# Chunked attention into a bilinear network: values, scores and sums of three units in one run on TensorE

## The chip, the cores and the metric

The kernel runs on one core of a Trainium2 chip. The metric is device time in microseconds (us) of one execution; the median of several runs is compared. Below, "the profile" is one execution recorded instruction by instruction, with times in us from the start of its span.

## What is computed

The reference, cut to what matters (8 batches, 8 heads, 576 tokens each, head size 64; 4608 tokens in all, model width 512, inner width 1536):

```python
# attention inside chunks of 64 tokens
scores = (1 / sqrt(64)) * q_c @ k_c.T            # per head and chunk, 64 x 64
attn = exp(scores - max) ; attn /= attn.sum(-1)
x = (attn @ v_c), heads side by side             # 4608 x 512
# bilinear network
a = x @ w_a ; b = x @ w_b                        # 512 x 1536 each
out = (a * b) @ w_out                            # 4608 x 512
```

## The kernel before, in words

**Blocks, units, groups.** The tokens are cut into 9 blocks of 512 (K = 0 to 8), each of two units of 256 tokens (U = 0 to 17; block K has units 2K and 2K+1). Attention is done unit by unit, the network block by block. Blocks 0 and 1 take their own path at the start; from block 2 on each block goes through six groups (K,i), i = 0 to 5, one for each 256 columns of w_a and w_b. The order of every engine's instructions is written out by hand in the program: what follows in the text follows in the engine's queue.

**Attention of a unit** has four steps. `scores` (L266): 64 small matmuls (64x64) on the transposed q and k in `qkt` into two banks of PSUM, then Exp on ScalarE into `E` (of the two Exp the first follows at once, the second is put off to `exps`). `sums` (L296): four matmuls with a stationary block of ones give the sum over each chunk, spread over the rows; ScalarE takes Ln into `ln`. `inverse` (L317): ScalarE takes exp(-ln), one instruction over 128x1024. `values` (L324): 64 small matmuls of v and E; VectorE multiplies by the inverse and writes x (tile `xT`, L344). These small matmuls use quarters of TensorE's array (64*64 in the profile); all others use the whole array (128*128). The banks of values and of sums come from the pool `pt` by default; scores may be given a pool.

**A group** makes a and b for 256 columns with seven products in place of eight (a Strassen-Winograd scheme): p1, p6, p2, p5, p7, p3, p4 (L460 to L493), each four matmuls of 128x256 (`product`, L446). p1 fills bank A (pool `pa`); ScalarE copies A into bank B (`pb`, two banks in turn, L464); p6 adds to B, ScalarE copies B to u; p2 adds to A, copied to b; p5 adds to B, copied to v (L457). p7 fills C (`pc`). Then `add7` (VectorE, L484 and L485): c = C + v, and C = C + u in PSUM. p3 adds to B, and VectorE multiplies B by b; p4 adds to C, and VectorE multiplies C by c (L496); the products a*b go to `ab_sb`. The products need sums and differences of weights (t1 to t4) and of x (s1 to s4, `combine_x`, L412, four VectorE instructions a block: s1 and s2 and s3 and s4).

p3 and p4 of a group are issued during the next one, so TensorE's order in the loop (L892 to L935) is: p1 of this group, an out part, p3 of the last, p6 of this, p4 of the last, p2 of this, an out part, p5, p7. Attention steps stand in two places, after p3 (`attend(K, i, 0)`) and before p5 (`attend(K, i, 1)`); the table `attention` (L845 to L872) says which step where.

**The output of a block** (`OutGroup`, L537) is made in the next block by the same scheme: parts n0 to n6, each in two halves (th = 0, 1) of six matmuls. n0 and n1 fill bank A (`po`), copied to bank B (`pq`) by ScalarE after n0 and scaled into the first half of o0 after n1 (L612); n2, n3 and n5 add to B, which goes to u, v and the second half of o0 (L617, L620, L624); n4 and n6 fill C (`po`): after n4 VectorE scales C + v into o1 and then adds u to C in PSUM (L637, L641), after n6 it scales C into o1 (L630). `chunks` (L879) says how many halves stand in each of a group's two places. They need sums of `ab_sb`, made by `combine_ab` (L508) on GpSimd: three parts for each of j = 0, 1, 2 (j = 0 in group 4, j = 1 in group 5, j = 2 in group 0 of the next block), then part 3 for all j.

**Inputs.** `bring(U)` (L363): GpSimd casts q and k of unit U, SP issues the loads of the next unit and then the transposing DMAs of q and k into `qkt`, GpSimd casts v. SP also issues the stores. The staging tiles have 8 buffers, `raw`, `qkt` 3, `E`, `ln` and the out tiles 2.

Of the kernel before, what the change touches and what calls it, by code (L numbers as in the profile page):

```python
# [16 lines left out]
def kernel(  # L17
# [275 lines left out]
            late.pop(0)()  # L293
            n -= 1

    def sums(U, halves=None):  # L296
        E = E_of[U]
        sm = [bank() for _ in range(2)]
        for cl in range(2):
            for j in range(2):  # L300
                nc.tensor.matmul(  # L301
                    sm[cl][j * 64:j * 64 + 64, :],
                    ones[cl * 64:cl * 64 + 64, :],
                    E[cl * 64:cl * 64 + 64, j].rearrange("p m g s -> p (m g s)"),
                    start=True,
                    stop=True,
                )
        ln_of[U] = sm_pool.tile([128, 2, NKT, 128], FP32, name="ln")
        rs_of[U] = ln_of[U]
        for cl in range(2):  # L310
            nc.scalar.activation(
                out=ln_of[U][:, cl].rearrange("p m n -> p (m n)"), in_=sm[cl], func=AF.Ln
            )
            if halves:
                inverse(U, cl)

# [43 lines left out]
        if f is not None:  # L360
            values(f)

    def bring(U):  # L363

        if U >= NU:
            return
        cast(U, "qk")
        load(U + 1, "q" if U < 9 else "qkv")
        transpose_dma(U)
        bring_v(U)  # L370

    def bring_v(U):
        cast(U, "v")
        if U < 9:
            load(U + 1, "kv")
# [33 lines left out]

    s_of = {}  # L410

    def combine_x(K, parts=(0, 1, 2, 3)):  # L412
        xT = x_tiles[K]
        x11, x12 = xT[:, 0:2, 0:256], xT[:, 2:4, 0:256]
        x21, x22 = xT[:, 0:2, 256:512], xT[:, 2:4, 256:512]
        if K not in s_of:
            s_of[K] = [s_pool.tile([128, 2, 256], FP16, name=f"s{j}") for j in range(1, 5)]
        s1, s2, s3, s4 = s_of[K]
        for part in parts:
            o, x0, x1, op = (  # L420
                (s1, x21, x22, ADD),
                (s2, s1, x11, SUB),
                (s3, x11, x21, SUB),
                (s4, x12, s2, SUB),
            )[part]
            nc.vector.tensor_tensor(out=o, in0=x0, in1=x1, op=op)

    class Group:

# [107 lines left out]
    class OutGroup:  # L537
# [20 lines left out]
        def part(self, n, th):  # L558
# [28 lines left out]
            for cols in (slice(0, 128), slice(128, 256)) if end else [slice(0, 256)]:  # L587
                for kt in range(HFT):
                    nc.tensor.matmul(  # L589
                        t[:, c0:c0 + 256][:, cols],  # L590
                        a[:, kt, th * 128:th * 128 + 128],
                        w[:, kt, cols],
                        start=n in (0, 4) and first and kt == 0,
                        stop=last and kt == HFT - 1,
                        skip_group_check=True,
                    )
                if end:
                    nc.vector.tensor_scalar(
                        out=rows(self.o1, cols), in0=self.C[:, cols], scalar1=OUT_SCALE,
                        scalar2=None, op0=MULT,  # L600
                    )
                    store(
                        self.K, 1, th, self.o1[:, th], cols, nc.scalar if cols.start else nc.sync
                    )
            if not last or end:
                return
            if n == 0:
                self.B = self.bank(1)
                nc.scalar.copy(out=self.B, in_=self.A)
            elif n == 1:  # L610
                self.o0 = self.tile_of(0)
                nc.scalar.activation(  # L612
                    out=rows(self.o0, lo), in_=halves(self.A), func=AF.Copy, scale=OUT_SCALE
                )
            elif n == 2:
                self.u = self.temp("uo_sb")
                nc.scalar.copy(out=self.u, in_=self.B)  # L617
            elif n == 3:
                self.v = self.temp("vo_sb")
                nc.scalar.activation(out=self.v, in_=self.B, func=AF.Copy, scale=OUT_SCALE)  # L620
            elif n == 4:
                self.o1 = self.tile_of(1)
            elif n == 5:
                nc.scalar.activation(  # L624
                    out=rows(self.o0, hi), in_=halves(self.B), func=AF.Copy, scale=OUT_SCALE
                )
                for c in [th] if one else range(2):
                    store(self.K, 0, c, self.o0[:, c])
            else:
                nc.vector.tensor_scalar(  # L630
                    out=rows(self.o1, lo), in0=halves(self.C), scalar1=OUT_SCALE,
                    scalar2=None, op0=MULT,
                )
                for c in [th] if one else range(2):
                    store(self.K, 1, c, self.o1[:, c], lo if one else slice(0, DM))
            if n == (3 if one else 4):
                nc.vector.scalar_tensor_tensor(  # L637
                    out=rows(self.o1, hi), in0=halves(self.C), scalar=OUT_SCALE,
                    in1=halves(self.v), op0=MULT, op1=ADD,
                )  # L640
                nc.vector.tensor_tensor(out=self.C, in0=self.C, in1=self.u, op=ADD)  # L641
                if one:
                    store(self.K, 1, th, self.o1[:, th], hi)

# [27 lines left out]
    with tc.manual_schedule(  # L672
# [174 lines left out]
        def at(K, i, n, f, u):  # L847
            if u < NU:
                attention.setdefault((K, i, n), []).append(lambda: f(u))

        def scores_beside(pool):
            return lambda u: scores(u, (pool, psum_b[0]), 1)

        for K in range(2, NBLK):
            U = 2 * K + 2
            if K == 2:
                at(K, 0, 0, lambda u: combine_x(2, (2, 3)), U)
                at(K, 0, 0, scores, U)
                at(K, 0, 1, sums, U)
            else:  # L860
                attention[K, 0, 0] = [lambda K=K: combine_x(K, (2,))]
                attention[K, 0, 1] = [lambda K=K: combine_x(K, (3,))]
                at(K, 0, 0, sums, U)
            at(K, 1, 0, inverse, U)
            at(K, 2, 1, values, U)
            at(K, 2, 1, scores_beside(psum_o), U + 1)
            at(K, 3, 0, sums, U + 1)
            at(K, 3, 1, inverse, U + 1)
            at(K, 4, 1, values, U + 1)
            at(K, 4, 1, scores_beside(psum_q), U + 2)  # L870
            at(K, 5, 0, lambda u: combine_x(u // 2, (0,)), U + 1)
            at(K, 5, 1, lambda u: combine_x(u // 2, (1,)), U + 1)  # L872

        def attend(K, i, n):
            for f in attention.get((K, i, n), ()):
# [2 lines left out]
        last = None  # L878
        chunks = {  # L879
            2: (1, 1, 1, 1, 1, 2, 1, 2, 3, 0, 1, 1),  # L880
            4: (1, 1, 1, 1, 2, 1, 1, 2, 2, 0, 1, 1),
            NBLK - 1: (1,) * 12,
        }

# [7 lines left out]
        for K in range(2, NBLK):  # L892
            for i in range(NWP):
                if i == (2 if K == 2 else 1):
                    for j in range(3):
                        combine_ab(K - 1, 3, j)
                if i == 1:
                    bring(2 * K + 4)
                elif i == 3 and K > 2:
                    bring(2 * K + 5)  # L900
                elif i == 3:
                    cast(9, "qk")
                    load(10)
                    transpose_dma(9)
                if i == 0:
                    g = OutGroup(K - 1)
                    outs += [
                        lambda g=g, n=n, th=th: g.part(n, th) for n in range(7) for th in range(2)
                    ]
                now = Group(K, i)  # L910
                now.p1()
                if last:
                    last.add7()
                chunk(chunks.get(K, chunks[4])[2 * i])
                if K == 2 and i == 0:
                    for j in range(3):
                        combine_wo(3, j)
                if last:
                    last.p3()
                attend(K, i, 0)  # L920
                now.p6()
                if last:
                    last.p4()
                    finish(last)
                if K == 2 and i < 3:
                    combine_w(i + 3, 3)
                if K == 2 and i == 4:
                    cast(9, "v")
                now.p2()
                chunk(chunks.get(K, chunks[4])[2 * i + 1])  # L930
                attend(K, i, 1)
                now.p5()
                exps()
                now.p7()
                last = now  # L935
        ends = [
# [46 lines left out]
```

The softmax here doesn't subtract the row's maximum and nothing guards it: scores larger than these inputs give would overflow.

## Time and profile before

| | us |
|---|---|
| median of 8 runs (lowest, highest) | 303.99 (303.34, 306.97) |
| the profiled execution's own time | 304.43 |
| its span | 302.6 |
| TensorE busy in the span | 292.9 |
| VectorE, ScalarE, GpSimd busy | 210.1, 196.3, 192.4 |
| mean granted TensorE clock | 0.994 of full speed |
| mean of one: p1 to p7 matmul (128x256) | 0.273 |
| ScalarE copy of a bank (L457, `u_sb`) | 0.588 |
| VectorE multiply out of a bank (L496) | 0.689 |
| GpSimd `combine_ab` (first part) | 1.182 |

A timeline line gives start, duration, engine, line of the program, operation, what is written <- what is read, shapes and count, and in brackets how long the engine was idle before it and what ended that. Instructions on one engine overlap a little at their ends, so the distance of two starts can be less than the first one's duration; a matmul's end is modelled, and the distance of starts is its cost. PE is TensorE, DVE VectorE, ACT ScalarE, POOL GpSimd, SPq the queue of DMA issues on SP. Six groups make a block, some 30 us: block 5 begins near 172, block 6 near 202.

### The profile page before, as it was taken

What the parts mean: (1) busy time and instruction counts of PE and PEld (TensorE: products, weight loads), DVE (VectorE), ACT (ScalarE), POOL (GpSimd) and SP (SyncE); (2) the same over time, 40 slices, a digit from 0 to 9 for tenths busy, and PEclk for the clock granted to TensorE, in tenths of its full rate; (3) what the DMA queues carried; (4) which work ended last, traced back from release to release, by engine and by line L of the source; (5) the groups of instructions that cost most, each with busy time, mean ns of one, the idle gap of its engine ahead of it and who ended that gap; (6) DMA issues with size and microseconds to landing.
All of it is one profiled execution on the core that took longest, in us unless ns stands there. A gap on an engine that the chain in (4) does not pass through costs nothing.

```text
span 302.6 us, 8607 instructions
## 1 busy us (share of the span) xinstructions
PE 292.9 (97%) x3525; PEld 232.4 (77%) x3527; DVE 210.1 (69%) x343; ACT 196.3 (65%) x355; POOL 192.4 (64%) x180
## 2 busy tenths in 40 slices
PE   6799999999999999999999999999999999999995
PEld 2344567766588888888888888888888888888884
DVE  3457767858567696769667966786679667965773
ACT  2643567358487768776867687768776876566622
POOL 0567657999799488818881888179717901780650
PEclk9899999999999999999999999999999999999999
DMA  7999999989999979899859386948723001100024
GB/s 226 283 374 363 310 295 364 255 187 187 243 234 245 216 175 269 182 223 227 204 133 255 110 203 139 221 150 192 124 61 88 11 2 69 73 1 2 2 104 173
DMA packets 141159, 54.29 MB, mean 179 GB/s; under 512 B 117184, under 2 KB 135232, under 8 KB 141120
## 3 DMA queue, kind: packets, MB, share of 16 engines
q1 hardware_dynamic: 140976, 53.69, 70.2%
q8 instruction: 27, 0.44, 0.6%
q14 instruction: 12, 0.10, 0.1%
q10 hardware_dynamic: 144, 0.07, 0.1%
HBM read 37.75 MB, written 9.44 MB: 156 GB/s over the span
## 4 chain that ended last, share of the span: by engine, by line
PE 90%; DVE 4%; DMA 2%; ACT 1%; issue 1%; SPq 1%; POOL 0%; DVEq 0%; ACTq 0%
PE pb L446 18%; PE pc L446 12%; PE pa L446 12%; PE po L589 12%; PE pq L589 10%; PE po L396 3%; PE pc L396 3%; PE pb L396 3%; PE pb L662 3%; DMA st<-in_k_dram 2%; PE pa L396 2%; PE pq L396 2%; PE pt L334 2%; PE pt L301 2%; PE pc L101 1%
## 5 line engine op out<-in xcount | busy, mean ns | idle before, releaser
L526 POOL TENSOR_TENSOR so<-ab_sb 128x512 f16<-128x512 f16 x23 | 27.2, 1182 | 68.7 <-DVE ab_sb L496 68.7
L446 PEld LDWEIGHTS <-t 128*128 128x128 f16 x504 | 48.2, 98 | 8.8 <-issue 2.3
L446 PE MATMUL pb<-s,wa 128*128 128x256 f16 x336 | 50.6, 273 | 0.0
L446 PE MATMUL pa<-xT,wb 128*128 128x256 f16 x336 | 50.4, 273 | 0.0
L484 DVE TENSOR_TENSOR c_sb<-pc,v_sb 128x512 f32<-128x512 f32 x42 | 28.9, 687 | 29.8 <-ACT v_sb L457 29.8
L589 PEld LDWEIGHTS <-ab_sb 128*128 128x128 f16 x390 | 37.7, 98 | 5.3 <-issue 0.9
L446 PEld LDWEIGHTS <-wb 128*128 128x128 f16 x336 | 32.8, 98 | 4.1
L446 PEld LDWEIGHTS <-wa 128*128 128x128 f16 x336 | 31.7, 98 | 4.3 <-issue 0.2
L496 DVE SCALAR_TENSOR_TENSOR ab_sb<-pc,c_sb 128x512 f16<-128x512 f32 x42 | 29.0, 689 | 7.7 <-PE pc L446 6.3
L457 ACT COPY u_sb<-pb 128x512 f32<-128x512 f32 x42 | 24.7, 588 | 14.9 <-PE pb L446 14.7
L496 DVE SCALAR_TENSOR_TENSOR ab_sb<-pb,b_sb 128x512 f16<-128x512 f32 x42 | 28.9, 689 | 6.1 <-PE pb L446 5.2
L464 ACT COPY pb<-pa 128x512 f32<-128x512 f32 x42 | 24.1, 573 | 10.6 <-PE pa L446 10.3
L589 PEld LDWEIGHTS <-so 128*128 128x128 f16 x288 | 28.1, 98 | 3.4
L457 ACT COPY b_sb<-pa 128x512 f32<-128x512 f32 x42 | 25.0, 595 | 7.1 <-PE pa L446 7.1
L485 DVE TENSOR_TENSOR pc<-pc,u_sb 128x512 f32<-128x512 f32 x42 | 28.9, 688 | 0.0
L526 POOL TENSOR_TENSOR so<-so,ab_sb 128x512 f16<-128x512 f16 x23 | 27.0, 1172 | 1.7
L457 ACT COPY v_sb<-pb 128x512 f32<-128x512 f32 x42 | 24.7, 587 | 5.1 <-PE pb L446 4.4
L526 POOL TENSOR_TENSOR ab_sb<-ab_sb 128x512 f16<-128x512 f16 x23 | 26.7, 1163 | 0.0
L526 POOL TENSOR_TENSOR so<-ab_sb,so 128x512 f16<-128x512 f16 x23 | 26.1, 1161 | 0.0
L446 PE MATMUL pc<-s,t 128*128 128x256 f16 x168 | 25.2, 273 | 0.2 <-DVE ab_sb L496 0.2
L446 PE MATMUL pb<-s,t 128*128 128x256 f16 x168 | 25.3, 273 | 0.0
L446 PE MATMUL pc<-xT,t 128*128 128x256 f16 x168 | 25.2, 273 | 0.1
(129 smaller groups left out, 570.5 us busy)
## 6 DMA issues: line engine op xcount, KB each, us to landing
st<-in_v_dram SPq DMA_DIRECT2D x32, 256.0 KB, 4.7
out_dram<-o_sb SPq DMA_DIRECT2D x30, 256.0 KB, 2.4
st<-in_k_dram SPq DMA_DIRECT2D x22, 256.0 KB, 4.3
st<-in_q_dram SPq DMA_DIRECT2D x20, 256.0 KB, 3.7
st<-in_q_dram SPq DMA_DIRECT2D x6, 512.0 KB, 6.1
st<-in_moe_w_b_dram SPq DMA_DIRECT2D x6, 512.0 KB, 6.6
st<-in_moe_w_a_dram SPq DMA_DIRECT2D x6, 512.0 KB, 6.6
st<-in_moe_w_out_dram SPq DMA_DIRECT2D x6, 512.0 KB, 7.2
```

Source lines behind the costliest of these rows:

```text
L301: nc.tensor.matmul(sm[cl][j * 64:j * 64 + 64, :], ones[cl * 64:cl * 64 + 64, :], E[cl * 64:cl * 64 + 64, j].rearrange("p m g s -> p (m g s)"),
L334: nc.tensor.matmul(av[cl][j * 64:j * 64 + 64, m, g, :], vr[cl * 64:cl * 64 + 64, g, 2 * m + j, :], E[cl * 64:cl * 64 + 64, j, m, g, :], st ...
L396: nc.tensor.matmul(ps[n], w_ab[n, i][:, kt, o:o + 128], xT[:, kt, c0:c1], start=(kt == 0), stop=(kt == NKT - 1),)
L446: nc.tensor.matmul(t[:, h * 256:h * 256 + 256], w[:, kt, h * 128:h * 128 + 128], x[:, kt], start=start and h == 0 and kt == 0, stop=h == 1 ...
L457: nc.scalar.copy(out=t, in_=src)
L464: nc.scalar.copy(out=self.B, in_=self.A)
L484: nc.vector.tensor_tensor(out=self.c, in0=self.C, in1=self.v, op=ADD)
L485: nc.vector.tensor_tensor(out=self.C, in0=self.C, in1=self.u, op=ADD)
L496: nc.vector.scalar_tensor_tensor(out=self.dst[:, :, c0:c0 + 256], in0=t.rearrange("p (h n) -> p h n", h=2), scalar=AB_SCALE, in1=o.rearran ...
L526: (eng or nc.gpsimd).tensor_tensor(out=o, in0=x0, in1=x1, op=op)
L589: nc.tensor.matmul(t[:, c0:c0 + 256][:, cols], a[:, kt, th * 128:th * 128 + 128], w[:, kt, cols], start=n in (0, 4) and first and kt == 0, ...
L662: nc.tensor.matmul(out_ps[K, tg], ab_tiles[K][:, ft, tg * 128:tg * 128 + 128], wo_sb[:, ft], start=(ft == 0), stop=(ft == NFT - 1),)
```

## The change

Where things stand in a block before and after (units of block K's table: U = 2K+2):

| step | before, blocks 3 to 8 | after, blocks 4 to 8 |
|---|---|---|
| (K,0) | sums(U) after p3 | nothing |
| (K,1) | inverse(U) after p3 | inverse(U) before p5, after the out part n1 |
| (K,2) before p5 | values(U), scores(U+1) | values(U), scores(U+2), sums(U+1) |
| (K,3) | sums(U+1) after p3, inverse(U+1) before p5 | inverse(U+1) before p5 |
| (K,4) before p5 | values(U+1), scores(U+2) | values(U+1), scores(U+3), sums(U+2) |
| (K,5) | combine_x of the next block, parts 0 and 1 (VectorE; 2 and 3 in the next group) | combine_x, all four parts, on GpSimd |

Steps of units beyond 17 fall away. Block 3 keeps its old places, and gets scores(11) and sums(10) before p5 of (3,5), in banks of `pq`, `pb` and `pt`. Block 2 keeps its own as well, but the sums of x for block 3 go to GpSimd. In the new runs scores use banks of `pc` and `pb`, sums banks of `pa` and `po` or `pq`; of their two Ln only that of `pa` follows at once, the other comes after p1 of the next group (`late_ln`). In (K,2) and (K,4) of blocks 4 to 7 one out half stands behind p5, ahead of p7, a place that was empty before. Before, (K,2), (K,3) and (K,4) had two, one and two halves after p1 and one, two and none before p5; after, they have one each after p1, one each before p5, and in (K,2) and (K,4) the one behind p5. Out parts go in the order 0, 1, 2, 3, 5, 4, 6 from block 4 on. Casts, loads and transposes follow the scores, one unit earlier from block 4 on: unit 11 in (3,3) as before, unit 12 in (3,4), then 2K+5 in (K,1) and 2K+6 in (K,3), with the casts of v apart in groups 2 and 3. In the out parts u is scaled when it is copied, and added in the last scaling of C in place of the add in PSUM.

```diff
-    def sums(U, halves=None):
+    late_ln = []
+
+    def sums(U, halves=None, pools=(None, None)):
...
-        sm = [bank() for _ in range(2)]
+        sm = [bank(p) for p in pools]
...
+        ln = ln_of[U]
         for cl in range(2):
-            nc.scalar.activation(
-                out=ln_of[U][:, cl].rearrange("p m n -> p (m n)"), in_=sm[cl], func=AF.Ln
+            late_ln.append(
+                lambda cl=cl: nc.scalar.activation(
+                    out=ln[:, cl].rearrange("p m n -> p (m n)"), in_=sm[cl], func=AF.Ln
+                )
             )
+        for cl in range(1 if pools[0] else 2):
+            late_ln.pop(0)()
...
-            nc.vector.tensor_tensor(out=o, in0=x0, in1=x1, op=op)
+            (eng or nc.vector).tensor_tensor(out=o, in0=x0, in1=x1, op=op)
...
-                self.u = self.temp("uo_sb")
-                nc.scalar.copy(out=self.u, in_=self.B)
+                self.u = self.temp("uo_sb")
+                nc.scalar.activation(out=self.u, in_=self.B, func=AF.Copy, scale=OUT_SCALE)
...
-                nc.vector.tensor_scalar(
-                    out=rows(self.o1, lo), in0=halves(self.C), scalar1=OUT_SCALE,
-                    scalar2=None, op0=MULT,
+                nc.vector.scalar_tensor_tensor(
+                    out=rows(self.o1, lo), in0=halves(self.C), scalar=OUT_SCALE,
+                    in1=halves(self.u), op0=MULT, op1=ADD,
                 )
...
-                nc.vector.tensor_tensor(out=self.C, in0=self.C, in1=self.u, op=ADD)
...
+        def sums_beside(pool):
+            return lambda u: sums(u, pools=(psum_a, pool))
+
         for K in range(2, NBLK):
             U = 2 * K + 2
             if K == 2:
...
+            elif K == 3:
+                at(K, 0, 0, sums, U)
+            at(K, 1, 1 if K > 3 else 0, inverse, U)
+            at(K, 2, 1, values, U)
+            if K < 4:
+                at(K, 2, 1, scores_beside(psum_o), U + 1)
+                at(K, 3, 0, sums, U + 1)
             else:
...
+                at(K, 2, 1, scores_beside(psum_c), U + 2)
+                at(K, 2, 1, sums_beside(psum_o), U + 1)
             at(K, 3, 1, inverse, U + 1)
             at(K, 4, 1, values, U + 1)
...
+            if K < 4:
+                at(K, 4, 1, scores_beside(psum_q), U + 2)
+            else:
+                at(K, 4, 1, scores_beside(psum_c), U + 3)
+                at(K, 4, 1, sums_beside(psum_q), U + 2)
+            at(K, 5, 0, lambda u: combine_x(u // 2, (0, 1, 2, 3), nc.gpsimd), U + 1)
+            if K == 3:
+                at(K, 5, 1, scores_beside(psum_q), U + 3)
+                at(K, 5, 1, sums, U + 2)
...
-            4: (1, 1, 1, 1, 2, 1, 1, 2, 2, 0, 1, 1),
+            3: (1, 1, 1, 1, 2, 1, 1, 2, 2, 0, 1, 1),
+            4: (1, 1, 1, 1, 1, (1, 1), 1, 1, 1, (1, 1), 1, 1),
...
                 if i == 1:
-                    bring(2 * K + 4)
-                elif i == 3 and K > 2:
-                    bring(2 * K + 5)
+                    bring(2 * K + 4 if K < 4 else 2 * K + 5, "qkv" if K < 4 else "qk")
+                elif i == 2 and K > 3:
+                    cast(2 * K + 4, "v")
+                elif i == 3 and K < 4:
+                    bring(2 * K + 5, "qk" if K == 2 else "qkv")
                 elif i == 3:
...
+                    cast(2 * K + 5, "v")
+                    bring(2 * K + 6, "qk")
+                elif i == 4 and K == 3:
+                    bring(12, "qk")
...
-                        lambda g=g, n=n, th=th: g.part(n, th) for n in range(7) for th in range(2)
+                        lambda g=g, n=n, th=th: g.part(n, th)
+                        for n in (range(7) if K < 4 else (0, 1, 2, 3, 5, 4, 6))
+                        for th in range(2)
...
                 now.p1()
+                while late_ln:
+                    late_ln.pop(0)()
                 if last:
                     last.add7()
...
                 attend(K, i, 1)
                 now.p5()
                 exps()
+                chunk(c2)
                 now.p7()
```

## The prediction

> **What bounds the kernel now.** I read the page first: busy time, then the chain that ended last.
>
> ```profile
> PE 292.9 (97%) x3525; PEld 232.4 (77%) x3527; DVE 210.1 (69%) x343; ACT 196.3 (65%) x355; POOL 192.4 (64%) x180
> PE 90%; DVE 4%; DMA 2%; ACT 1%; issue 1%; SPq 1%; POOL 0%; DVEq 0%; ACTq 0%
> ```
>
> TensorE is on 90% of the chain, so in the steady part a microsecond taken from TensorE, or a wait put into it, goes straight into the time. Next I read its timeline through block 6, where the change acts (the four `ones` matmuls are sums(14)):
>
> ```profile
> 202.19 0.60 PE L446 MATMUL pb<-s,wa 128*128 128x256 f16 x4
> 202.72 0.41 PE L301 MATMUL pt<-E,ones 64*64 64x512 bf16 x4
> 203.06 0.61 PE L446 MATMUL pb<-s,t 128*128 128x256 f16 x4
> 203.51 0.60 PE L446 MATMUL pc<-xT,t 128*128 128x256 f16 x4
> ...
> 208.75 0.82 PE L589 MATMUL po<-wo,ab_sb 128*128 128x256 f16 x6
> 209.41 0.60 PE L446 MATMUL pb<-s,wa 128*128 128x256 f16 x4
> ...
> 210.72 1.47 PE L589 MATMUL pq<-wot,so 128*128 128x256 f16 x12
> 212.03 0.60 PE L446 MATMUL pb<-s,wa 128*128 128x256 f16 x4
> ```
>
> Starts are 0.44 us apart per product of 4 matmuls and 0.655 per out part of 6: nothing waits. The second half is the end of group (6,1): n1 (208.75), p5, p7, then p1 of (6,2), both n2 parts, and p3 at 212.03. Here is what ScalarE and VectorE do beside it:
>
> ```profile
> 207.03 1.06 ACT L320 ACTIVATE ln<-ln 128x1024 f32<-128x1024 f32 x1
> 208.12 0.58 ACT L457 COPY u_sb<-pb 128x512 f32<-128x512 f32 x1
> 208.95 0.58 ACT L457 COPY b_sb<-pa 128x512 f32<-128x512 f32 x1 [0.24 <-PE pa L446]
> 209.61 0.60 ACT L612 ACTIVATE o_sb<-po 128x512 f32<-128x512 f32 x1
> 210.10 0.58 ACT L457 COPY v_sb<-pb 128x512 f32<-128x512 f32 x1
> 210.92 0.57 ACT L464 COPY pb<-pa 128x512 f32<-128x512 f32 x1 [0.24 <-PE pa L446]
> ```
> ```profile
> 211.32 0.69 DVE L485 TENSOR_TENSOR pc<-pc,u_sb 128x512 f32<-128x512 f32 x1
> ```
>
> The inverse (207.03) now sits where the next copy is not due for 1.09 us. The v copy at 210.10 opens two things: p3 may write its bank, and VectorE may make c (210.71, so 0.03 after v's end) and then C+u (211.32, over at 212.01), which p4 of (6,1) needs. p4 comes at 212.90 because two n2 parts lie in front of p3.
>
> **Part 1, three units in one run: gain.** sums(14) displaces the work around it by 203.51 - 202.19 - 0.875 (two products) = 0.445 us. Its four matmuls run together. By the groups of TensorE, 512 columns take 408 ns and 64 take 197, so 0.47 ns a column and 0.24 us for 512; the other 0.2 us is the change of tiling before and after (bounds 0.15 and 0.23). Runs from block 3 on: before, four in each of blocks 3 to 7, so 20; after, five in block 3 (one new: scores(11) and sums(10) at (3,5)), two in each of blocks 4 to 7, so 13. Seven fewer at 0.2: **-1.4 us**. The matmuls are the same.
>
> **Part 2, the inverse moves from before p3 of (K,1) to after n1: loss.** In blocks 4 to 7 ScalarE's order becomes b, o_sb (waits for n1), inverse, v, copy A to B. I lay it out with t = 0 at the start of p5 (209.41 above). o_sb starts at 0.20 and the next instruction 0.49 later: inverse at 0.69. How long the inverse holds the queue is seen earlier, at 86.34, where the ready u copy follows it after 0.96: v starts at 1.65 and ends at 2.23. One of the two n2 parts has also moved behind p2, so p3 is due at 1.97 (three products and 0.655). p3 of (K,1), and with it all of TensorE's queue, waits to 2.28 (a consumer started 0.05 after its releaser at 110.60), ends at 2.72. The A-to-B copy ends at 2.70, p6 runs 2.75 to 3.19. c starts at 2.26, C+u at 2.87 and ends at 3.56: p4 at 3.61, due at 2.84. So 0.77 in each of four blocks: **+3.1 us**. A rule bears on this: the Trainium skill, TensorE: Matmul & The Clock Gate, section Architectural detail, says that ScalarE takes its queue strictly first in, first out, whereas TensorE may pull weight loads ahead. By it v stands behind the inverse: +3.1. If a ready v could pass it, 0. The row at 87.30 speaks for the rule: that copy's product was over at 86.54 and it still began only when the inverse let go. Bounds per block 0.5 and 0.9.
>
> The second inverse stays at (K,3) after one part (n5) where two stood: b at -0.46, inverse 0.01, v 0.97 to 1.55, C+u over at 2.88, p4 due 2.84: 0.09 by four, **+0.4** (0 to 0.8).
>
> **Part 3, the merged runs themselves.** Behind such a run ScalarE has Exp of pc, Ln of pa, v, Exp of pb, copy, Ln of the third bank. Counted from p5: 0, 0.50, 1.0, 1.5, then the copy at 2.21 when p1 (moved to 1.97 by the part behind p5) is over, done at 2.78; p6 is due at 3.06. p7 needs pc at 1.09 and gets it at 0.65. The run itself wants pc 1.46 after p4 began to end, with VectorE's multiply done by 0.95, and pa with about 0.5 to spare. So nothing, covered by 0.3 to 0.5 us; each 0.1 beyond that costs 0.7 over the runs. In (K,4) the part behind p5 is n4's second half, ending at 1.09; VectorE's scaling of it (0.69, starts 0.25 after as at 190.91) is over at 2.03, while n6, which writes that bank, is due at 1.97: 0.11 by four, **+0.4** (0 to 0.8).
>
> **Part 4, the hand-over (3,5).** No part stands behind p5 here and both Ln come at once: Exp -0.05, Ln 0.45 and 0.94, v 1.43 to 2.01, Exp of pb 1.89 to 2.51, the copy (same bank, so it waits for the end) 2.54 to 3.11. p3 due 1.97 goes at 2.06, p6 due 2.50 at 3.16: **+0.75** (0.3 to 1.0). And scores(11) moves from (4,2) to (3,5), due at 139.9. Its transposed k, whose issue stays behind the load of unit 12 on SP:
>
> ```profile
> L254 SPq DMA_TRANSPOSE qkt<-k_raw x1: 1254/1254/1254, 136.4 to 136.4; - x1
> DMA to landing us min/median/max: 4.3/4.3/4.3
> ```
>
> lands at 140.7: **+0.8** (0, if it comes a little sooner; 2.3, if the load of unit 13, which now follows at once instead of two stores, slows it, or if landing counts from the issue's end). The stores of o0 and o1 that stood there now go out behind the load of 13 and the transposes of 12, at about 146.2 to 148; landing in 2.4 (median of the DMA table) they are done by 150.4 at the latest, o0's by 149.2, and ScalarE writes that buffer again behind n1 at about 150: covered by under 1 us, and a miss would hold ScalarE's queue for the difference, once. From block 4 on loads, transposes and the v casts keep their distance to their takers within one group; 4 us and more are left.
>
> **Part 5, sums of x on GpSimd.** VectorE loses four instructions a block, which wait for GpSimd at times: 0.41 alone, up to 1.27 beside it. One held a multiply, and TensorE with it:
>
> ```profile
> 108.68 1.27 DVE L426 TENSOR_TENSOR s<-xT 128x512 f16<-128x512 f16 x1
> 109.87 0.68 DVE L496 SCALAR_TENSOR_TENSOR ab_sb<-pc,c_sb 128x512 f16<-128x512 f32 x1
> ...
> 110.60 0.60 PE L446 MATMUL pc<-s,t 128*128 128x256 f16 x4 [0.17 <-DVE ab_sb L496]
> ```
>
> p7 started 0.77 after the product before it, not 0.44: **-0.33**. GpSimd gets 4 x 1.16 = 4.6 us a block, on 19.6 of 30. In its queue they stand behind combine_ab j=0 (over at 199.1 for block 6, with x ready at 196.9): s2 done at 201.4, needed at 202.6 or later. For block 3: behind the cast over at 109.6, s2 done at 112.0, needed at 112.7. Behind them combine_ab j=1, j=2, the three of part 3 and the casts move by 4.6; the first taker, n2, has 1.4 us left (block 3: 0.3), the transposes on SP 4. So nothing; without that cover it costs what it is late, five times. The Trainium skill, SBUF — State Buffer, lists one exclusive port pair for VectorE (with two SBUF inputs) and GpSimd: by it the move ends a contention; by the durations alone, 1.16 against 0.41, it would be a loss of 3 us a block. It is off TensorE's path either way.
>
> **Part 6, u in the last scaling.** One VectorE add (0.69) less per out group; the scaling with a third operand has the duration of the plain one (L637 0.69, L630 0.69). At the very end 0.42 and 0.28 stay as they are. 0 (-0.1 to +0.1).
>
> **Sum.** -1.4 - 0.33 + 3.1 + 0.4 + 0.4 + 0.75 + 0.8 = +3.7 us. The profiled execution took 304.43 (span 302.6 and 1.8 around it), giving 308.1; the median of the runs, 303.99, is 0.44 below it: **307.7 us**.
>
> **Rivals.** (a) ScalarE's lateness is covered: the inverse in (K,1) and the copies at (3,5) are through before TensorE comes. Then -1.73 + 0.8 remain: 303.1, not slower. It decides where v ends before 1.92 instead of 2.23 and C+u before 2.79 instead of 3.56, so if the inverse holds the queue under 0.2 us. For it: ScalarE is only 65% busy. Against: 0.96 at 86.34. (b) GpSimd comes late: if its queue runs 2 us behind my count, s2 or n2 wait some 0.6 us in five blocks: 310.7. For it: 81% load from block 4 on; against: idle stretches of 7.9 us before combine_ab j=0 at 165.61. (c) The hand-over is longer, unit 11's transposes landing at 142.2: 309.2. (d) The order in the built kernel is as described, so "it does not do what it says" is out.
>
> **Chances.** Forecast 0.64 (own range 305.8 to 308.8), (a) 0.18, (b) 0.08, (c) 0.10. About 0.5% (1.5 us) is what a measurement here can tell from no change. (a) spreads 0.08 to faster by more than that and 0.10 to within it; the forecast's lower tail gives 0.06 more to within. Range 304.5 to 310.0: it leaves out most of (a) and the far end of (b).
>
> **What would show it.** In the changed profile: in blocks 4 to 7 p4 of (K,1) starting 1.64 after p1 of (K,2) and the n2 part are over, where 0.87 is two products, with C+u as its releaser; the inverse directly between o_sb and v; one 0.44 sums run gone per unit; a TensorE gap at about 139.9 that a transpose ends; p7 at 110.3 without a gap. If v ends before p3 is due, the largest term is wrong and the sign with it.

## The result, and the profile after

| | before | after |
|---|---|---|
| median, us (lowest, highest; runs) | 303.91 (303.19, 306.97; 32) | 307.59 (306.81, 311.19; 11) |
| the profiled execution, its span | 304.43, 302.6 | 311.36, 309.6 |

The ratio is 1.0148, 95% interval 1.0123 to 1.0173: slower by 3.7 us, which is where the forecast lay. But the times after stand in two groups, six from 306.8 to 307.6 and five from 308.8 to 311.2, and the profiled execution (311.36, not counted among the eleven) belongs to the upper one. The forecast does not explain that group.

First the page of after: busy time and the chain.

```profile
PE 296.0 (96%) x3525; PEld 233.4 (75%) x3527; DVE 192.6 (62%) x310; ACT 195.9 (63%) x355; POOL 218.1 (70%) x204
PE 70%; DMA 7%; DVE 6%; ACT 5%; SPq 5%; POOL 4%; issue 2%; ACTq 0%; DVEq 0%; POOLq 0%
```

The chain was 90% TensorE; now a fifth of the span has gone over to DMA, VectorE, ScalarE, SP and GpSimd. TensorE waits, and the chain follows what it waits for. (The program's lines stand 2 to 8 further down after: L446 is L454, L589 is L597, L485 is L493, L612 is L620.)

**The inverse at its new place**, TensorE in block 5: n2, p3, p6, p4, p2, n2, then the merged run (values, scores, two pairs of sums), and p5.

```profile
186.40 0.82 PE L597 MATMUL pq<-wot,so 128*128 128x256 f16 x6
187.36 0.60 PE L454 MATMUL pb<-s,wa 128*128 128x256 f16 x4
187.85 0.60 PE L454 MATMUL pb<-s,t 128*128 128x256 f16 x4
188.69 0.60 PE L454 MATMUL pc<-xT,t 128*128 128x256 f16 x4 [0.25 <-DVE pc L493]
...
189.56 0.82 PE L597 MATMUL pq<-wot,so 128*128 128x256 f16 x6
190.31 0.45 PE L341 MATMUL pt<-E,v_raw 64*64 64x64 bf16 x32
190.87 0.41 PE L303 MATMUL pa<-E,ones 64*64 64x512 bf16 x2
...
191.22 0.61 PE L454 MATMUL pb<-s,wa 128*128 128x256 f16 x4
```

ScalarE beside it:

```profile
185.29 0.60 ACT L620 ACTIVATE o_sb<-po 128x512 f32<-128x512 f32 x1
185.79 1.05 ACT L327 ACTIVATE ln<-ln 128x1024 f32<-128x1024 f32 x1
186.73 0.58 ACT L465 COPY v_sb<-pb 128x512 f32<-128x512 f32 x1
```

From n2 to p3 it is 0.96 where 0.655 is the work: 0.30 of waiting. (A gap is counted here as the distance of two starts less the work; the figure in brackets in a profile line is the idle time alone and can be smaller.) p3 to p6 takes 0.49 (0.05 too long), p6 to p4 0.84 (0.40 too long). Together 0.75, and the same three gaps stand in blocks 5 to 7, and in block 4 with a longer one at p3. ScalarE shows why: the product that v copies was issued at 185.09, but v starts only when the inverse lets go, at 186.73; it ends at 187.31, and p3 starts 0.05 later. p4 follows C+u (VectorE, L493, 187.95 to 188.64), again by 0.05. A page's label alone would not tell this: p3 carries no bracket at all here.

**Block 4 has more.** The same n2 and p3, a block earlier:

```profile
152.32 0.82 PE L597 MATMUL pq<-wot,so 128*128 128x256 f16 x6
155.40 0.60 PE L454 MATMUL pb<-s,wa 128*128 128x256 f16 x4 [2.26 <-ACT v_sb L465]
```

ScalarE, SP's queue, and the stores of this stretch (issue durations, then the time from issue to landing):

```profile
153.33 0.60 ACT L620 ACTIVATE o_sb<-po 128x512 f32<-128x512 f32 x1 [2.19 <-DMA out_dram<-o_sb]
```
```profile
144.47 2.09 SPq L254 DMA_TRANSPOSE qkt<-q_raw  x1
146.65 1.25 SPq L254 DMA_TRANSPOSE qkt<-k_raw  x1
148.00 2.04 SPq L541 DMA_DIRECT2D out_dram<-o_sb  x4
```
```profile
L541 SPq DMA_DIRECT2D out_dram<-o_sb x4: 408/448/538, 148.0 to 149.6; - x4
DMA to landing us min/median/max: 2.5/4.7/4.9
```

The name on TensorE's wait, v, is only the last link. v stood behind the inverse, the inverse behind o_sb, and o_sb stood 2.19 waiting for the store of the block before out of the same tile. The stores of this stretch were issued from 148.0 on, behind the load of unit 13 and the transposes of unit 12. Before, they went out from 137.7 on:

```profile
137.72 4.16 SPq L533 DMA_DIRECT2D out_dram<-o_sb  x4
DMA to landing us min/median/max: 2.0/2.5/3.5
```

Their landing, too, took up to 4.9 after, against 3.5 at most before.

After that wait the clock of TensorE fell. Stretches of 2 us: length, busy time (and instructions) of PE, PEld, DVE, ACT and POOL, then the granted clock, the DMA share and GB/s:

```profile
155.00:157.00 2.00, 1.36 (x11) 1.02 (x11) 1.62 (x3) 1.05 (x3) 2.00 (x4) 1.00 0.88 200
157.00:159.00 2.00, 2.00 (x11) 1.38 (x10) 0.95 (x2) 0.95 (x2) 1.01 (x2) 0.50 1.11 252
159.00:161.00 2.00, 2.00 (x75) 1.31 (x73) 0.73 (x2) 0.96 (x3) 0.66 (x1) 0.65 1.26 264
```

From 157.0 to 160.4 the granted clock was 0.50. TensorE is busy throughout, but with 11 matmuls in the first 2 us where 20 or 21 are usual. p4 to p5 of this group took 4.02 us; where the store is not waited for (the run with the stores first, below) the same stretch takes 2.53. So this low stretch costs 1.49, on top of 2.1 for the wait at p3 beyond its ordinary 0.30.

**The hand-over (3,5)**: the first score matmuls of unit 11, and p6 of this group in the next one.

```profile
140.96 0.22 PE L274 MATMUL pq<-qkt 64*64 64x64 bf16 x2 [0.87 <-DMA qkt<-k_raw]
...
144.66 0.61 PE L454 MATMUL pb<-s,t 128*128 128x256 f16 x4 [0.51 <-ACT pb L472]
```

The transposed k came 0.87 late, and p6 started 1.10 after p3 (143.56) where 0.44 is the work: 0.66 for ScalarE's queue. The p7 near 110 that had waited for VectorE now starts at 110.42, 0.44 after the product before it: that 0.33 is saved.

The account, on the profiled executions (in brackets what the prediction put):

| term | us |
|---|---|
| seven fewer runs of small matmuls, 7 x 0.245 | -1.7 (-1.4) |
| p7 near 110 | -0.33 (-0.33) |
| inverse of (K,1): 4 x 0.75 | +3.0 (+3.1) |
| inverse of (K,3): 4 x 0.10 | +0.4 (+0.4) |
| n4 to n6: 4 x 0.07 | +0.3 (+0.4) |
| hand-over, ScalarE and transposes | +0.66 + 0.87 (+0.75 + 0.8) |
| store of o0 in block 4, wait and slow clock, 2.1 + 1.49 | +3.6 (0) |
| start of the span a little later | +0.2 (0) |
| sum | +7.0 (+3.7) |

Measured +6.9. The 0.245 of a run: the separate sums and the values with scores displaced 0.445 and, in the mean of seven runs (0.77 to 0.89), 0.82 us of TensorE before, 1.26 together; the merged run displaces 1.02.

### The profile page after: what moved, and what is told of

Same layout as the page of the kernel before. It is cut to its first block, busy times and chain, and to the rows that moved or that the text cites. A ratio compares the mean times of both kernels' runs of the same rounds, so it can differ in the third digit from the quotient of the medians.

```text
span 309.6 us, 8593 instructions
## 1 busy us (share of the span) xinstructions
PE 296.0 (96%) x3525; PEld 233.4 (75%) x3527; DVE 192.6 (62%) x310; ACT 195.9 (63%) x355; POOL 218.1 (70%) x204
## 4 chain that ended last, share of the span: by engine, by line
PE 70%; DMA 7%; DVE 6%; ACT 5%; SPq 5%; POOL 4%; issue 2%; ACTq 0%; DVEq 0%; POOLq 0%
PE pb L454 12%; PE pc L454 9%; PE po L597 9%; PE pa L454 9%; PE pq L597 7%; SPq L188 4%; PE po L404 3%; PE pc L404 3%; DMA st<-in_k_dram 3%; PE pb L404 3%; PE pb L669 3%; DMA st<-in_v_dram 2%; ACT ln L327 2%; PE pa L404 2%; PE pq L404 2%
## 5 line engine op out<-in xcount | busy, mean ns | idle before, releaser
L534 POOL TENSOR_TENSOR so<-ab_sb 128x512 f16<-128x512 f16 x23 | 26.5, 1153 | 44.2 <-DVE ab_sb L504 44.2
L454 PEld LDWEIGHTS <-t 128*128 128x128 f16 x504 | 48.7, 98 | 9.8 <-issue 2.7
L454 PE MATMUL pb<-s,wa 128*128 128x256 f16 x336 | 50.6, 273 | 2.7 <-ACT v_sb L465 2.3
L454 PE MATMUL pa<-xT,wb 128*128 128x256 f16 x336 | 50.9, 274 | 0.0
L597 PEld LDWEIGHTS <-ab_sb 128*128 128x128 f16 x390 | 37.7, 98 | 5.6 <-issue 0.9
L454 PEld LDWEIGHTS <-wa 128*128 128x128 f16 x336 | 31.6, 98 | 9.2 <-issue 5.4
L454 PEld LDWEIGHTS <-wb 128*128 128x128 f16 x336 | 33.0, 98 | 4.3
L597 PEld LDWEIGHTS <-so 128*128 128x128 f16 x288 | 28.3, 99 | 3.8
L493 DVE TENSOR_TENSOR pc<-pc,u_sb 128x512 f32<-128x512 f32 x42 | 29.0, 689 | 0.0
L351 DVE TENSOR_TENSOR xT<-pt,ln 128x512 f16<-128x512 f32 x29 | 18.8, 686 | 13.0 <-PE pt L341 10.1
L454 PE MATMUL pc<-xT,t 128*128 128x256 f16 x168 | 25.4, 274 | 1.1 <-DVE pc L493 1.0
L219 POOL CAST q_raw<-st 128x1024 bf16<-128x1024 f32 x17 | 17.6, 1036 | 11.9 <-DMA st<-in_q_dram 11.9
```

The source lines that it names most:

```text
L219: eng.tensor_copy(out=raw[n, U], in_=staged.pop((n, U)))
L351: nc.vector.tensor_tensor(out=x.rearrange("p m (g c s) -> p m g c s", g=2, c=2)[:, m, :, cl, :], in0=av[cl][:, m], in1=rs[:, cl, m].rearra ...
L454: nc.tensor.matmul(t[:, h * 256:h * 256 + 256], w[:, kt, h * 128:h * 128 + 128], x[:, kt], start=start and h == 0 and kt == 0, stop=h == 1 ...
L534: (eng or nc.gpsimd).tensor_tensor(out=o, in0=x0, in1=x1, op=op)
L597: nc.tensor.matmul(t[:, c0:c0 + 256][:, cols], a[:, kt, th * 128:th * 128 + 128], w[:, kt, cols], start=n in (0, 4) and first and kt == 0, ...
```

## Experiments

My theory: the terms of the table are separate places that add up, the largest by far the inverse, and the upper group is the store. The rivals: the merged runs themselves cost time, through what they queue on ScalarE; or the waits stand in for each other, so that taking one away only uncovers the next.

### The inverse of (K,1) back behind p3

```diff
-            at(K, 1, 1 if K > 3 else 0, inverse, U)
+            at(K, 1, 0, inverse, U)
```

> The changed kernel with one thing undone: in blocks 4 to 7 the inverse stands again after p3 of (K,1) instead of behind n1. Theory (the inverse stands between o_sb and the v copy on ScalarE, so p3 waits 0.30 and p4 another 0.45 in each of four blocks, as the changed kernel's trace has it): the gaps at p3 and p4 vanish in blocks 5 to 7, and the time falls by 4 x 0.75 = 3.0 us from 307.6 to about 304.6. Rival 1 (the loss comes from ScalarE's backlog behind the merged runs, and the inverse only meets it): the inverse finds the same backlog in its old place, u is late instead, and the time stays within 1 us of 307.6. Rival 2 (the sums of x on GpSimd are what costs): unchanged at 307.6.

306.99 (303.83 to 308.14, 8 runs; before 303.93), ratio 1.0082 (1.0051 to 1.0112): a miss by 2.4. The gaps at p3 and p4 are gone from blocks 5 to 7, as the theory has it. In block 4 they are not, and ScalarE says why:

```profile
153.87 0.60 ACT L620 ACTIVATE o_sb<-po 128x512 f32<-128x512 f32 x1 [2.67 <-DMA out_dram<-o_sb]
```

The store holds the queue with or without the inverse behind it, and p3, p6 and p4 of block 4 wait 2.4 in all. The transposes of unit 11 came 1.44 late here too. In the profile of the kernel with both edits below these two waits are nothing and 0.81, which makes 3.0 less; its profiled execution, 304.29 against 307.19 here, took 2.9 less. I had left the store out of the expectation, as a matter of the profiled execution only. The times suggest that it is there in most executions of this kernel, though only one was profiled: one alone, 303.83, lies where it should without it.

### Unit 12's transposes and the load of unit 13 behind the stores of o0

```diff
-                    bring(12, "qk")
+                    cast(12, "qk")
+                elif i == 5 and K == 3:
+                    transpose_dma(12)
+                    load(13)
```

> The changed kernel with one thing moved: in block 3 the load of unit 13 and the transposes of unit 12 are issued on SP behind the stores of o0 instead of ahead of all four stores (the casts of unit 12 stay where they are). Theory (the upper group of the changed kernel's times, 309 to 311 against 307, is the write of o0 in block 4 that waits for the store of its buffer, 2.19 us in the profile, and the TensorE clock that falls to half after it): the wait on the store is gone in block 4, p3 of (4,1) waits 0.3 as in blocks 5 to 7, all times lie within 1 us of 307, the profiled run too. Rival (the spread has another cause, such as the transposes of unit 11): still a group of times 2 to 4 us above the rest.

307.26 (306.56 to 309.18, 6 runs), ratio 1.0111 (1.0086 to 1.0136). In the profile o_sb of block 4 goes without a wait, p3 waits 0.29 as in the other blocks, and the clock stays at 1.00. The transposes of unit 11, untouched in their place, were at most 0.1 late here. One time, 309.18, lies outside what I expected. Its mean granted clock was 1.00, so it had no low stretch; it was not profiled, and its cause is open.

### Both

The two edits above together:

```diff
-            at(K, 1, 1 if K > 3 else 0, inverse, U)
+            at(K, 1, 0, inverse, U)
...
-                    bring(12, "qk")
+                    cast(12, "qk")
+                elif i == 5 and K == 3:
+                    transpose_dma(12)
+                    load(13)
```

> The changed kernel with the inverse of (K,1) behind p3 again and unit 12's transposes and the load of unit 13 behind the stores of group 5. Theory (the terms are separate and add): 307.3 less 4 x 0.75 = 304.3, with only the hand-over's waits left at (3,5), and no wait of o_sb for a store. Rival (the wait for the store and the inverse's are one cost that stands in for the other): no better than 306.5.

304.29 (303.52 to 305.89, 13 runs; before 303.87), ratio 1.0014 (1.0003 to 1.0026). Against the one edit less (307.26) this is 2.97 = 4 x 0.74 (2.95 by the two ratios, as the chips differ): with the store out of the way the inverse is worth just what its gaps in the trace say. These two terms add. In block 5 p3, p6 and p4 follow n2 without a gap:

```profile
181.59 0.82 PE L597 MATMUL pq<-wot,so 128*128 128x256 f16 x6
182.24 0.60 PE L454 MATMUL pb<-s,wa 128*128 128x256 f16 x4
182.68 0.60 PE L454 MATMUL pb<-s,t 128*128 128x256 f16 x4
183.12 0.60 PE L454 MATMUL pc<-xT,t 128*128 128x256 f16 x4
```

What is left in the profile is the hand-over: 0.81 for unit 11's transposes and 0.67 for ScalarE.

### A third tile for out, and its control

The two kernels keep the order of every instruction of the changed kernel. The first has three out tiles instead of two, so o_sb of block 4 writes a tile whose store is long done; to make room, both have seven staging tiles in place of eight.

```diff
-    st_pool = ctx.enter_context(tc.tile_pool(name="st", bufs=8))
+    st_pool = ctx.enter_context(tc.tile_pool(name="st", bufs=7))
...
-    o_pool = ctx.enter_context(tc.tile_pool(name="osb", bufs=2))
+    o_pool = ctx.enter_context(tc.tile_pool(name="osb", bufs=3))
```

> The changed kernel with three tiles for out instead of two, and seven instead of eight staging tiles to make room; the order of every engine's instructions is the same. In block 4 ScalarE then writes a tile whose store is long done. Theory (the wait for the store of o0 makes the times near 310): no wait of o_sb in block 4, a profile without the 2.2 us wait and the low clock behind it, and times at 306.5 to 307.5 with none above 308.5. Rival (the spread has another source, such as the transposes of unit 11): times above 309 go on, the median unchanged or higher.

> The control for the third out tile: the changed kernel with seven staging tiles and two out tiles. Theory: as the changed kernel, a median of 307 to 308.5 with some times at 309 to 311, and in the profile a wait of o_sb for the store in block 4 wherever its time is above 308.5. Rival (the eighth staging tile is what matters): the same times as with three out tiles.

With three: 307.73 (306.99 to 308.32, 4 runs), ratio 1.0127 (1.0107 to 1.0147), a little above what I expected, but with no time over 308.5. The control: 311.86 (310.40 to 312.23, 4 runs), ratio 1.0255 (1.0232 to 1.0279). ScalarE in block 4, first with three tiles, then the control:

```profile
151.76 0.60 ACT L620 ACTIVATE o_sb<-po 128x512 f32<-128x512 f32 x1
```
```profile
154.93 0.60 ACT L620 ACTIVATE o_sb<-po 128x512 f32<-128x512 f32 x1 [1.92 <-DMA out_dram<-o_sb]
```

This is the closest pair for the upper group: one order, one chip, all times of the one under 308.4 and all of the other over 310.3, and the only edit between them is the third tile. But the store is not all that differs in their profiles. The control lies 3.4 above the top of what I expected, and its profile says what came together: the store (1.85 more at p3), transposes of unit 11 that were 1.91 late (1.67 with three tiles), and behind the latter 3.4 us at half clock (143.3 to 146.7), which the stretch from 143 shows as a mean of 0.58:

```profile
143.00:145.00 2.00, 2.00 (x13) 1.48 (x12) 0.54 (x1) 1.97 (x5) 2.00 (x3) 0.58 1.04 236
```

The slow matmuls are worth 1.66 by the distances of starts, but in them disappears the 0.67 for which p6 waits on ScalarE with three tiles, so the low clock costs 1.0. Here one loss did stand in for another. Of the 3.3 us between the two profiled executions the store is thus a little over half. The rival (transposes make the spread) is not wholly out: they vary from execution to execution, but they were almost as late in the kernel that stayed low. Why all four times of the control lie above most of the changed kernel's is open.

### Parts of the change in the kernel before

The inverse at its new place for K > 3, where both n2 halves still lie ahead of p3:

```diff
-            at(K, 1, 0, inverse, U)
+            at(K, 1, 1 if K > 3 else 0, inverse, U)
```

> The kernel before with one thing of the change: in blocks 4 to 7 the inverse stands before p5 of (K,1), behind n1, instead of after p3. Nothing is merged, and both n2 halves still lie in front of p3. Theory (v ends 2.23 after p5's start; with two n2 halves p3 is due at 2.62 and p4 at 3.50, C+u is over at 3.56): p3 does not wait, p4 waits 0.1 in each of four blocks: +0.4 us, 304.3. Rival 1 (the inverse ahead of v costs by itself, whatever lies in front of p3): +3.0 us, 306.9. Rival 2 (v may pass the inverse): 303.9.

304.05 (13 runs; before 303.93), ratio 0.9997 (0.9987 to 1.0007). In the profile p3 never waits and p4 waits 0.10 in each of blocks 4 to 7; of these 0.4 the median shows 0.1. So the move of the inverse costs next to nothing by itself. The kernel with both edits above is the other half: there the n2 half stays behind p2, the inverse is back, and p3, p6 and p4 of (K,1) have no gap. The 0.75 needs both moves together.

All sums of x on GpSimd:

```diff
-                attention[K, 0, 0] = [lambda K=K: combine_x(K, (2,))]
-                attention[K, 0, 1] = [lambda K=K: combine_x(K, (3,))]
...
-            at(K, 5, 0, lambda u: combine_x(u // 2, (0,)), U + 1)
-            at(K, 5, 1, lambda u: combine_x(u // 2, (1,)), U + 1)
+            at(K, 5, 0, lambda u: combine_x(u // 2, (0, 1, 2, 3), nc.gpsimd), U + 1)
```

> The kernel before with one thing of the change: all four sums of x of a block on GpSimd from (K,5), none on VectorE, from block 3's x on. Theory (VectorE's sum held the multiply in front of p7 of (2,5); nothing waits for GpSimd's sums): the 0.33 gap at 110 is gone, 303.6 us. Rival (GpSimd's queue gets late, 4.6 us more a block: s2 or n2 wait): 304.5 to 307, with waits on GpSimd at p6 of (K,0) or at n2.

303.49 (22 runs; before 303.93), ratio 0.9986 (0.9976 to 0.9996), no wait for GpSimd in the profile, and p7 near 110 in time: -0.4 against -0.33 in the sum.

u in the last scaling, as in the change (both scalings of C, and u scaled when copied):

```diff
-                nc.scalar.copy(out=self.u, in_=self.B)
+                nc.scalar.activation(out=self.u, in_=self.B, func=AF.Copy, scale=OUT_SCALE)
...
-                nc.vector.tensor_tensor(out=self.C, in0=self.C, in1=self.u, op=ADD)
```

> The kernel before with u added in the last scaling in place of PSUM, alone. Theory: VectorE loses one add per out group off the path, 304.0 within 0.2. Rival (the third operand makes the last scalings longer, or C comes free sooner for n6): 304.5 or more, or 303.5 or less.

303.86 (14 runs; before 303.87), ratio 0.9997 (0.9983 to 1.0010): nothing.

### The merged runs with every other loss repaired

From the changed kernel; the places that cost are put back or moved, the merged runs stay:

```diff
-            at(K, 1, 1 if K > 3 else 0, inverse, U)
+            at(K, 1, 0, inverse, U)
...
-                at(K, 5, 1, sums, U + 2)
+                at(3, 5, 1, lambda u: sums(u, pools=(psum_t, psum_t)), 10)
...
-            3: (1, 1, 1, 1, 2, 1, 1, 2, 2, 0, 1, 1),
+            3: (1, 1, 1, 1, 2, 1, 1, 2, 2, 0, 1, (0, 1)),
...
-                    bring(2 * K + 5, "qk" if K == 2 else "qkv")
+                    cast(11, "qk")
+                    transpose_dma(11)
+                    load(12)
+                    cast(11, "v")
...
+                elif i == 5 and K == 3:
+                    cast(12, "qk")
+                    transpose_dma(12)
+                    load(13)
```

The sums of x for block 4 are on VectorE as before.

> Merged runs kept; every place named for a loss put back: the inverse of (K,1) behind p3, unit 11's transposes ahead of the load of unit 12, unit 12's transposes and the load of unit 13 behind the stores, the sums of x for block 4 on VectorE, one Ln late and the last out half behind p5 at (3,5). My theory: the losses are these places and nothing in the merged runs, so what is left is the time before less 1.7 (seven runs at 0.245) and 0.3 (p7 at 110), plus some 0.7 (second inverse, n4 to n6): 302.6, ratio about 0.996. Rival (the merged runs themselves cost, by what queues behind them on ScalarE, or the store still waits): 304 or more. No wait over 0.5 in block 4 by my theory.

302.58 (302.30 to 303.52, 6 runs; before 303.87), ratio 0.9964 (0.9951 to 0.9977). This is faster than both kernels, by 1.3 and 5.0. No gap over 0.11 is left on TensorE from block 3 to block 7. The rival that the merged runs themselves cost falls.

### The same with the sums of units 11 to 17 apart

```diff
-                at(K, 2, 1, sums_beside(psum_o), U + 1)
+                at(K, 3, 0, sums, U + 1)
...
-                at(K, 4, 1, sums_beside(psum_q), U + 2)
+                at(K + 1, 0, 0, sums, U + 2)
```

> The repaired kernel with the sums of units 11 to 17 taken out of the merged runs, to stand behind p3 of (K,3) and of (K+1,0) as before; scores stay a unit ahead. Theory (each run of small matmuls costs 0.2 to 0.25 for the changes of tiling): seven runs more, the repaired kernel's time + 1.4 to 1.7. Rival (the gain of the merged runs is nothing, or it is given back on ScalarE): within 0.5 of the repaired kernel.

304.24 (304.06 to 304.81, 21 runs), ratio 1.0013 (1.0005 to 1.0021): 1.66 more than with the merged runs on the same chip, 0.237 a run. The work is the same; what differs is the number of changes between small and whole-array matmuls, and a little on ScalarE: p4 of (K,3) is 0.15 late where it was 0.10, in four blocks, 0.2 in all. Without that it is 0.21 a run.

### One step further: the inverse of (K,3) behind p3 too

```diff
-            at(K, 3, 1, inverse, U + 1)
+            at(K, 3, 0 if K > 3 else 1, inverse, U + 1)
```

> The repaired kernel with the inverse of (K,3) also behind p3, in the place that the sums left free, from block 4 on. Theory: the wait of 0.10 at p4 of (K,3) goes in four blocks, 302.6 less 0.4 = 302.2. Rival (the inverse then holds the u copy and p2 or p5 wait in its place): 302.6 or more.

303.28 (302.96 to 304.98, 22 runs; before 303.51), ratio 0.9988 (0.9978 to 0.9999): a miss, slower than the repaired kernel (0.9964) by some 0.7. ScalarE and TensorE in (5,3):

```profile
188.13 1.07 ACT L327 ACTIVATE ln<-ln 128x1024 f32<-128x1024 f32 x1
189.08 0.60 ACT L465 COPY u_sb<-pb 128x512 f32<-128x512 f32 x1
```
```profile
188.83 0.82 PE L597 MATMUL pq<-wo,so 128*128 128x256 f16 x6
189.73 0.60 PE L454 MATMUL pb<-s,wa 128*128 128x256 f16 x4
```

Now the u copy stands behind the inverse, and p5, which writes the bank that u is read from, waits 0.24. The 0.10 at p4 is gone, some 0.24 at p5 has come, in four blocks, and p7 of (4,0) waits 0.2 where it waited 0.05. ScalarE is late by now because the late Ln and an out copy are in front of it.

## Why the prediction came out as it did

**Largest term, right.** "The inverse moves from before p3 of (K,1) to after n1" was put at 4 x 0.77; the trace shows 0.75 a block, split as laid out (0.30, 0.05, 0.40), and 2.97 in all between two kernels that differ in this alone. The layout of ScalarE's queue, with 0.96 for the inverse's hold taken from these rows of the profile before, carried it:

```profile
86.34 1.06 ACT L320 ACTIVATE ln<-ln 128x1024 f32<-128x1024 f32 x1
87.30 0.58 ACT L457 COPY u_sb<-pb 128x512 f32<-128x512 f32 x1
```

After, the inverse held v for 0.94 (185.79 to 186.73), and p4 started 1.63 after p1 and the n2 part were over, where the sign named was 1.64. Rival (a), that the lateness is covered, falls. The run of the kernel before with the inverse moved adds what I had not said plainly: the cause is the cover lost with the n2 half.

**Gain of the runs, right or a little too small.** 0.2 a run against 0.245 in the trace and 0.21 to 0.237 between two kernels. I had read the 0.2 out of one run of sums alone.

**Hand-over, right in both parts**, 0.75 and 0.8 against 0.66 and 0.87. But the second is a spread and not a number: in the traces of kernels that keep unit 11's transposes in the place where the change has them they were 0.1, 0.81, 0.87, 1.44, 1.67 and 1.91 late. Rival (c), a landing at 142.2, is nearly reached in the control, at 141.9.

**Small terms** (second inverse, n4 to n6, sums of x, u) were right to within 0.2 each. With the sums of x on GpSimd VectorE was busy for 201.6 us instead of 210.1, and the loss of 3 us a block that the durations alone would give did not come; whether it was the port pair that had held VectorE's sums, no run here shows. Rival (b) falls: for block 3 s2 was done at 112.2 and needed at 112.8. It could be a little tighter in block 4: with the inverse back s2 was done at 143.6 and p6 due at 144.05. (The profile of that run names GpSimd's s as what p6 then waited for; but p6 reads s2, and the copy to its bank ended at 144.67, just before it started.)

**The step that failed** is the cover for the stores in part 4: "done by 150.4 at the latest, o0's by 149.2 ... covered by under 1 us, and a miss would hold ScalarE's queue for the difference, once", taken at 0 in the sum. The mechanism was named; its size was put at nothing. In the profiled execution it was 2.1, and 1.49 more for the clock. Two figures in it were off, and one thing was missing: the stores went out from 148.0, not 146.2, since the load and the transposes ahead of them kept SP's queue from 137.98 to 147.90; they landed in up to 4.9, where I took the DMA table's median of 2.4; and that the clock of TensorE could fall after such a wait was nowhere in the prediction. I should have carried a bound of some 2 us for the wait to the forecast.

So the match of the median, 307.59 to 307.7, is partly luck. The account without the store is +3.4, near 307.3, which is the lower group; the upper group is explained by that plus up to 3.6; and the median of eleven runs happens to be the highest of the lower group. The upper group is not one thing either. A stretch of 3.4 us at half clock lowers the mean granted clock of an execution to 0.994 (an estimate: half of 3.4 in some 305 us), and the two of its times at 308.84 and 310.24 have 0.999. So they had no low stretch, and must be up by waits alone; which ones, no profile shows. (An 0.994 does not say where the stretch lies: 307.28, in the lower group, has it too, and so has the profile before, at the start of its span.) What share of executions waits for the store, and why, is open too: going by the times alone, the control waits in all its executions, the kernel with a third tile in none, the changed kernel in about half.

## What to carry to other kernels

Before an instruction is moved on an in-order queue, write down for its new place what stands behind it and when each of these is due; and look whether the same change takes away the work that covered it, for here neither half of the pair cost more than 0.1 us in the median alone. Moving a prefetch ahead on a shared DMA queue moves every store behind it: ask which tile's next writer waits for that store, and count with the slowest landing in the trace, not the median. Merging runs of small matmuls was worth 0.2 to 0.25 us for each run saved here, and it was only kept when the places around it were laid out anew.

## What the runs showed of the hardware

- A run of 64x64 matmuls between whole-array ones cost 0.21 to 0.245 us beyond its matmuls. The Trainium skill, TensorEngine Tiling (Array Packing), section Key Properties, says that changing the tiling mode drains TensorE, without a price; the runs fit that and give a price, though no trace shows the drain itself.
- The granted clock fell to 0.50, for 3.4 us each time, after a wait with 2.26 us of idle (changed kernel, low from 157.0) and after one of 1.91 (control, low from 143.3), but not after 1.99 in the same control, 1.80 with the inverse back or 1.67 with three tiles. The profile of the kernel before has such a stretch at its start, 12.4 to 15.8, where no single idle time listed before it is over 1.3. The Trainium skill, TensorE: Matmul & The Clock Gate, section Part 1: The HAM clock gate, puts the half clock after at least one idle window of about 3.4 us that runs free of the kernel. The low stretches are as long as that window, but shorter idle times were enough here, and not always; what decides is not settled by these runs.
- The four stores of block 3's end landed in 2.0 to 3.5 us before and in 2.5 to 4.9 after, issued behind a load and two transposes; with the two of o0 ahead of these, 2.7 to 4.2. In the traces it is the place in the queue, 10 us later, that costs most, and the landing comes on top.
